# One row-tile block per chunk for all four strips, with the chunk's outputs in one run and PSUM banks chosen as the order is laid

## The chip, the cores and the metric

The kernel runs on one core of one Trainium2 chip. The metric is the device time of one execution in microseconds (us); lower is better. Work is spread over TensorE (PE, matmuls), VectorE (DVE), ScalarE (ACT), GpSimd (POOL) and the DMA queues, most of them issued by SyncE (SP). TensorE's products go to PSUM, which has eight banks of 512 float32 columns for 128 partitions.

## The reference

Four batches of 12800 rows with 128 channels pass an attention with 32 inducing points, twice (`mab`), and then a gated product with a causal depthwise convolution of five taps.

```python
def mab(q, kv):
    s = scale * (q @ kv.transpose(0, 2, 1))
    s = s - s.max(-1, keepdims=True)
    a = np.exp(s)
    a /= a.sum(-1, keepdims=True) + 1e-09
    return a @ kv
h = mab(I, x)          # I: the 32 inducing rows, softmax over the 12800 rows
x = mab(x, h)          # each row: softmax over 32 scores, then a @ h
...
for k in range(K):     # K = 5
    gate_pre += conv_w[k][None, None, :] * xp[:, k:k + S, :]
gate = 1.0 / (1.0 + np.exp(-gate_pre))
val = x @ w_val
return (gate * val @ w_out).astype(np.float32)
```

## The kernel before

**Tiling.** Each batch's 12800 rows are cut into four strips of 3200, and all strips are cut alike into chunks along the free dimension: eight chunks in batch 0 (128, 256, five of 512, 256 columns), seven in each other batch (448 and 480; batch 3 has 480, five of 512, 160). The 29 chunks are numbered 0 to 28 through the batches (`seqs`).

**Stages.** For each batch: first scores (`s1`, L422), maxima (`gm`), x transposed on TensorE where needed (`x`, L397), exponentials and sums of exp times x (`h`, L486), normalisation and folding of h into the weights (`u`, `t`, `w`, `W`, `po`; L528, L545, L565, L621, with cg, wf and w on GpSimd at L580 to L587). Then for each chunk: second scores (`s2`, L691) and their softmax over 32 (DVE, POOL and ACT), which ends in P1 and P2, the two float16 halves of the probabilities; GpSimd writes the second (L749, the P low half), with `sub` (L708) and `nm` (L731) before it. Since P has 32 values for a row, the gate and the value of a chunk are products of P with folded weights W of 32 x 128: for each strip fifteen gate matmuls (five taps, three products of halves each, L763) into a gate buffer in PSUM and three value matmuls (L772) into an 'a' bank. These are **row tiles**: the four strips lie on the four groups of 32 partitions and run beside each other. Scores and sums are **column tiles** (128 x 32), and outputs use the **full array**.

**After a block.** ScalarE takes the tanh of a pair of strips out of the gate buffer (tg, L833); VectorE multiplies it with the value in PSUM (gv, L843); ScalarE casts to a float16 half gh (L856), GpSimd takes the rest gl (L861); an output (`o`) is three full-array matmuls gh x wo, gh x wo, gl x wo (L884 to L886), for chunk 28 one in float32 (L877), then an eviction on VectorE (L899) or ScalarE (L901), by the list OUTV, and a store from SP (L920; L908 for chunk 28) or ACT (L914).

**Half blocks.** `rblock(k, half)` lays two half blocks for a chunk. In a half, one pair of strips (`ends`) finishes its gates while the other pair (`other`) does its three value units and begins its next gates; how many is chosen by a small dynamic programme (`begun`, with EVEN). A half that has values is written as two operations (`part(False)`, `part(True)`). There are 60 halves. The outputs of the pair that finished stand between halves.

**PSUM.** g0 and g1, the gate buffers of the two pairs, take two banks each with one buffer; the four 'a' banks hold scores, sums, values and outputs in turn: the k-th 'a' tile takes the bank of the (k-4)-th.

**The order.** Nothing is issued as it is written. Each step records an operation with its engine, an assumed duration, what it depends on and which tiles it makes and uses. ORDER, a list found by search, fixes TensorE's order. `lay` then lists the other engines' operations by assumed times, latest start first, shifted by a number for each function (URGE). `AHEAD` says how far loads run ahead, BUFS how many buffers each tile has. ("z", n, k) in ORDER stands for k matmuls of zeros into g1 (`idle`, L939), and eight more run at the start (L928, `warm_up`).

Of the kernel before, what the change touches and what calls it, by code (L numbers as in the profile page):

```python
# [20 lines left out]
P = 128  # L21
M = 32
R = 4
# [26 lines left out]
class Plan:  # L50
# [28 lines left out]
    def order(self, pe):  # L79
# [4 lines left out]
        for tag, made in self.tiles.items():  # L84
            bufs = BUFS[tag]
# [41 lines left out]
        for _ in range(PASSES):  # L127
            seq, at, end = self.lay(deps, succ, topo, nominal)
            if best is None or max(end) < best[0]:
                best = max(end), seq, at, end  # L130
            nominal = {b: end[a] for a, b in zip(pe, pe[1:])} | {pe[0]: 0.0}
        _, seq, self.at, self.end = best
# [3 lines left out]
    def lay(self, deps, succ, topo, nominal):  # L136
# [4 lines left out]
        for i in reversed(topo):  # L141
            late[i] = nominal.get(i, late[i])
            for s in succ[i]:
                late[i] = min(late[i], late[s] - ops[i]["dur"] - ops[i]["lag"])
        free, bus = {}, 1.45
# [9 lines left out]
        while len(seq) < n:  # L155
            best = None
            for e, lst in pools.items():
                if not lst:
                    continue
                start = max(free.get(e, 0.0), min(r for r, _ in lst))  # L160
                if best is None or start < best[0]:
                    best = (start, e)
# [6 lines left out]
            free[e] = end[i] - OVER.get(e, 0.0)  # L169
            if e == "SP":  # L170
                bus = max(bus, start) + ops[i]["dur"]
                end[i] = max(bus, start + 0.5) + (1.7 if start < 10.0 else 2.6)
                free[e] = start + 0.45
            seq.append(i)
# [9 lines left out]
        return seq, at, end  # L184


@functools.lru_cache(None)
def begun(n, units, even):


    last = len(n) - 1
    ways = {a: (a * n[0] + even * n[0] * (a - 6) ** 2, [a]) for a in range(units + 1)}
    for k in range(len(n)):
        more = {}
        for a, (c, way) in ways.items():
            for b in range(units + 1):
                first = max((units - a) * n[k], (3 * n[k - 1] if k else 0) + b * n[k]) + even * n[k] * (b - 6) ** 2
                for d in range(units + 1) if k < last else (0,):
                    second = max((units - b) * n[k], 3 * n[k] + (d * n[k + 1] if k < last else 0))
                    v = c + first + second + (even * n[k] * (d - 6) ** 2 if k < last else 0)  # L200
                    if d not in more or v < more[d][0]:
                        more[d] = v, way + [b, d]
        ways = more
    return min(ways.values())[1]
# [8 lines left out]
def tile_kernel(ctx: ExitStack, tc: tile.TileContext, xt, xk, indT_in, w64, out):  # L213
# [103 lines left out]
    def pt(key, shape=(P, 512), dt=F32):  # L317
        t = st[key] = psum.tile(list(shape), dt, name=key[0], tag=key[0], bufs=BUFS[key[0]])
# [457 lines left out]
    made = set()  # L776
# [330 lines left out]
```

## Time and profile before

| | us |
|---|---|
| three timed runs | 285.78, 286.11, 285.9 (median 285.9) |
| span of the profiled execution, first to last instruction | 284.3 |
| TensorE busy in it | 276.2 (97%) |
| VectorE, ScalarE, GpSimd busy | 232.2, 203.2, 214.0 |

The profiled execution has no timed duration of its own beside its span; the median of the timed runs is 1.6 us above it. Matmuls overlap, so a matmul's own duration is longer than the step from one to the next; the distance of two starts is what a matmul costs TensorE. The idle time in brackets is what an engine waited before a row, and the arrow names what ended it.

### The profile page before, as it was taken

To read this page: it belongs to the slowest core of one execution; us is meant where nothing else is said; L and a number is where in the kernel's file an instruction comes from. 1 tells how busy PE (TensorE), PEld (TensorE's weight loads), DVE (VectorE), ACT (ScalarE), POOL (GpSimd) and SP (SyncE) were. 2 spreads that over 40 slices of the span, in tenths; PEclk is the share of its full clock that TensorE was granted. 3 is DMA by queue.
4 is the path that set the end of the run, shared out by engine and by line. 5 is a ranking of instruction groups with operands and counts; after the bars stand their busy time and mean duration, and the time that the engine had idled before them with its cause. 6 is when DMAs were issued, how large, how long until landed. Compare 5 with 4: busy or idle time off the path is not lost.

```text
span 284.3 us, 9991 instructions
## 1 busy us (share of the span) xinstructions
PE 276.2 (97%) x4028; PEld 136.5 (48%) x4028; DVE 232.2 (82%) x577; ACT 203.2 (71%) x307; POOL 214.0 (75%) x256
## 2 busy tenths in 40 slices
PE   8899899999999999999999999999999999999992
PEld 3576547564343445555446445554444444333451
DVE  1694799999999989798898989877999977964571
ACT  2466162686884979787867599797778987888772
POOL 1122076998988789988798998989979979965680
PEclk9999999999999999999999999999999999999999
DMA  7999999979999879895999943144331343434445
GB/s 295 419 424 416 418 415 390 420 275 382 367 384 293 315 253 369 294 367 165 389 369 352 343 145 136 53 147 146 129 132 67 135 166 113 151 146 173 151 177 195
DMA packets 24351, 74.49 MB, mean 262 GB/s; under 512 B 2801, under 2 KB 12529, under 8 KB 22129
## 3 DMA queue, kind: packets, MB, share of 16 engines
q1 hardware_dynamic: 23872, 73.32, 68.2%
q8 instruction: 31, 0.51, 0.7%
q10 hardware_dynamic: 432, 0.54, 0.5%
q14 instruction: 16, 0.12, 0.1%
HBM read 47.63 MB, written 26.21 MB: 260 GB/s over the span
## 4 chain that ended last, share of the span: by engine, by line
PE 94%; DVE 2%; issue 1%; ACT 1%; POOL 0%; POOLq 0%
PE g L763 30%; PE a L884 9%; PE a L486 9%; PE a L691 8%; PE a L422 8%; PE a L772 8%; PE a L886 7%; PE a L885 7%; PE g L397 2%; PE g L939 2%; PE a L928 1%; PE a L621 1%; DVE ss L430 1%; PE a L528 1%; DVE os L899 0%
## 5 line engine op out<-in xcount | busy, mean ns | idle before, releaser
L861 POOL TENSOR_TENSOR gl<-tg,gh 128x1024 f16<-128x1024 f32 (+4 forms) x56 | 106.6, 1907 | 18.0 <-ACT gh L856 12.3
L763 PE MATMUL g<-P,W 32*128 32x448 f16 (+5 forms) x1740 | 109.7, 345 | 0.0
L833 ACT ACTIVATE tg<-g,gsc 128x1024 f32<-128x1024 f32 (+5 forms) x58 | 57.7, 995 | 32.3 <-PE g L763 29.0
L843 DVE SCALAR_TENSOR_TENSOR tg<-tg,a 128x512 f32<-128x512 f32 (+5 forms) x116 | 65.7, 603 | 10.2 <-PE a L772 8.7
L763 PEld LDWEIGHTS <-W 32*128 32x128 f16 x1740 | 51.0, 92 | 43.0 <-issue 13.2
L856 ACT CAST gh<-tg 128x1024 f16<-128x1024 f32 (+4 forms) x56 | 52.7, 942 | 0.8 <-PE a L885 0.8
L772 PE MATMUL a<-P,W 32*128 32x512 f16 (+5 forms) x348 | 43.1, 348 | 0.1
L901 ACT ACTIVATE os<-a,osc 128x448 f32<-128x448 f32 (+4 forms) x60 | 36.5, 632 | 6.2 <-PE a L886 5.7
L884 PE MATMUL a<-gh,wo 128*128 128x512 f16 (+4 forms) x112 | 40.1, 359 | 0.0
L885 PE MATMUL a<-gh,wo 128*128 128x512 f16 (+4 forms) x112 | 39.6, 354 | 0.0
L886 PE MATMUL a<-gl,wo 128*128 128x512 f16 (+4 forms) x112 | 39.6, 354 | 0.0
L899 DVE TENSOR_SCALAR os<-a,osc 128x448 f32<-128x448 f32 (+4 forms) x48 | 31.4, 670 | 9.6 <-PE a L886 9.4
L749 POOL TENSOR_TENSOR P<-pt,P 128x512 f16<-128x512 f32 (+4 forms) x29 | 29.9, 1037 | 1.8 <-ACT P L742 1.8
L731 POOL TENSOR_TENSOR e<-e,z 128x512 f32<-128x512 f32 (+4 forms) x29 | 27.1, 940 | 4.0 <-DVE z L723 2.8
L708 POOL TENSOR_TENSOR e<-e,m 128x512 f32<-128x512 f32 (+4 forms) x29 | 27.1, 939 | 3.9 <-DVE m L702 3.4
L486 PE MATMUL a<-xk,et 128*32 128x129 f32 x800 | 28.2, 275 | 0.7 <-DVE et L470 0.5
L422 PE MATMUL a<-xt,indT 128*32 128x512 f32 (+5 forms) x232 | 27.3, 538 | 0.0
L486 PEld LDWEIGHTS a<-xk,et 128*32 128x32 f32 x800 | 23.0, 109 | 8.6 <-issue 4.2
L691 PE MATMUL a<-xt,hT 128*32 128x512 f32 (+4 forms) x232 | 26.8, 544 | 0.0
L714 ACT ACTIVATE e<-e 128x512 f32<-128x512 f32 (+4 forms) x29 | 16.5, 572 | 10.6 <-POOL e L708 10.5
L430 DVE TENSOR_SCALAR_CACHE_REDUCE ss<-a 128x512 f32<-128x512 f32 (+5 forms) x29 | 17.1, 601 | 7.3 <-PE a L422 7.1
L884 PEld LDWEIGHTS <-wo 128*128 128x128 f16 x112 | 10.9, 97 | 25.0 <-issue 18.2
(108 smaller groups left out, 323.7 us busy)
## 6 DMA issues: line engine op xcount, KB each, us to landing
xt<-in_xt_dram SPq DMA_DIRECT2D x11, 1024.0 KB, 8.3
out_dram<-os SPq DMA_DIRECT2D x36, 256.0 KB, 3.6
xk<-in_xk_dram SPq DMA_DIRECT2D x10, 903.0 KB, 8.5
out_dram<-os SPq DMA_DIRECT2D x40, 224.0 KB, 2.6
xt<-in_xt_dram SPq DMA_DIRECT2D x8, 896.0 KB, 7.4
xk<-in_xk_dram SPq DMA_DIRECT2D x6, 1032.0 KB, 9.1
xt<-in_xt_dram SPq DMA_DIRECT2D x6, 960.0 KB, 7.8
xk<-in_xk_dram SPq DMA_DIRECT2D x5, 967.5 KB, 6.6
```

What stands on the lines that cost most here:

```text
L422: T.matmul(s[32 * r:32 * r + 32, :n], c_["indT"], x[:, o:o + n // 32, r, :], start=True, stop=True)
L486: T.matmul(t[32 * s:32 * s + 32, :P + 1], e[:, 32 * i:32 * i + 32], x[:, m + i, :], start=i < R, stop=i >= nb - R)
L691: T.matmul(s[32 * r:32 * r + 32, :n], st["hT", b], x[:, m:m + nb, r, :], start=True, stop=True)
L763: T.matmul(st[f"g{r // 2}", b, c][:, r % 2, :n], st["W", b][q, w, k, :], st[("P1", "P2")[e]][q, o:o + n], start=u == 0, stop=u == len(taps ...
L772: T.matmul(st["a", "v", b, c, r][:, :n], st["W", b][q, w, TAPS, :], st[("P1", "P2")[e]][q, o:o + n], start=u == 0, stop=u == 2)
L833: S.activation(t[:, :, :n], st[f"g{p}", b, c][:, :, :n], AF.Tanh, scale=st["gsc", b])
L843: V.scalar_tensor_tensor(t, t, 1.0, st["a", "v", b, c, r][:, :n], ALU.add, ALU.mult)
L856: S.copy(sb(pw, g1, [P, 2, 512], F16)[:, :, :n], st[tg][:, :, :n])
L861: G.tensor_tensor(sb(pw, g2, [P, 2, 512], F16)[:, :, :n], st[tg][:, :, :n], st[g1][:, :, :n], ALU.subtract)
L884: T.matmul(t, w[:, 0], st[g1][:, q, :n], start=True, stop=False)
L885: T.matmul(t, w[:, 1], st[g1][:, q, :n], start=False, stop=False)
L886: T.matmul(t, w[:, 0], st[g2][:, q, :n], start=False, stop=True)
```

## The change

- `rblock(k, *starts)` lays **one block for a chunk**, with the fifteen gate units of all four strips. The value units of the chunk before stand inside it: for the first pair of strips after `starts[0]` gate units, for the second after `starts[1]`. The block is cut at these places into operations of their own. Both tanh of the chunk come after the block's end. There are 30 blocks.
- An **'a' bank is chosen while the order is laid**: `lay` keeps a list of open banks with the time at which each comes free, gives a TensorE operation the earliest, and holds the operation back if there are too few.
- ORDER, URGE (now with a number for every function) and OUTV are new tables. The four outputs of a chunk stand mostly together. Twenty of the 21 matmuls of zeros stand in the middle of the order.
- AHEAD 25 to 12; buffers: xt 11 to 10, tg 3 to 4, gh 2 to 4, gl 2 to 3.
- The instructions are otherwise the same in kind and number, apart from two evictions that go from VectorE to ScalarE and one store that goes from SP to ACT.

```diff
+        wants = [[] for _ in range(n)]
+        held = {}
+        holds = [[] for _ in range(n)]
+        for i, key in self.tiles.get("a", []):
+            wants[i].append(key)
+            held[key] = 1 + len(self.users[key])
+            for u in [i] + self.users[key]:
+                holds[u].append(key)
+        open_ = [(0.0, b) for b in range(BUFS["a"])]
...
+                if e == "PE":
+                    w = len(wants[lst[0][1]])
+                    if w > len(open_):
+                        continue
+                    if w:
+                        start = max(start, open_[w - 1][0])
...
-        tag=key[0], bufs=BUFS[key[0]])
+        tag = f"a{plan.bank[key]}" if key[0] == "a" else key[0]
...
-    def rblock(k, half):
-        ends, other = ((0, 1), (2, 3)) if half == 0 else ((2, 3), (0, 1))
-        cur = seqs[k] if 0 <= k < len(seqs) else None
-        val = (seqs[k - 1] if k else None) if half == 0 else cur
-        nxt = cur if half == 0 else (seqs[k + 1] if k + 1 < len(seqs) else None)
...
+    def rblock(k, *starts):
+        cur = seqs[k] if k < len(seqs) else None
+        val = seqs[k - 1] if k else None
+        line = {r: [(gate_mm, *cur, r, u) for u in range(len(taps))] if cur else [] for r in range(R)}
+        cuts = [0, len(taps)]
+        if val:
+            for r in range(R):
+                at = starts[r // 2] if cur else 0
+                line[r][at:at] = [(val_mm, *val, r, u) for u in range(3)]
+            cuts = [0] + [at + d for at in sorted(starts) for d in (0, 3)] + [len(line[0])] if cur else [0, 3]
...
+        for lo, hi in zip(cuts, cuts[1:]):
+            todo = [line[r][s] for s in range(lo, hi) for r in range(R)]
...
+            i = PE(max(spent), f, list(dict.fromkeys(deps)), new, use, "rows", 0.34)
...
 ORDER = [
...
-    ("o", 26, 0), ("r", 28, 0), ("o", 26, 2), ("o", 26, 3), ("r", 28, 1), ("r", 29, 0), ("o", 28, 0), ("o", 27, 1),
...
+    ('o', 25, 0), ('o', 24, 1), ('o', 25, 2), ('r', 28, 6, 12), ('o', 25, 1), ('o', 26, 1), ('r', 29, 1, 12),
...
-AHEAD = 25
+AHEAD = 12
-BUFS = dict(xt=11, ..., tg=3, gh=2, gl=2, ...
+BUFS = dict(xt=10, ..., tg=4, gh=4, gl=3, ...
```

ScalarE near the end of the program, before (tanh L833 of one pair of a chunk of 512, cast to gh L856, output eviction L901; g_ and a number is one gate buffer):

```order
L856 CAST gh<-tg 128x1024
L833 ACTIVATE tg<-g_5290,gsc 128x1024
L901 ACTIVATE os<-a,osc 128x512 x2
L856 CAST gh<-tg 128x1024
L833 ACTIVATE tg<-g_5349,gsc 128x1024
```

And ScalarE there after (the same three operations are L827, L850 and L895):

```order
L827 ACTIVATE tg<-g_5337,gsc 128x1024
L827 ACTIVATE tg<-g_5340,gsc 128x1024
L850 CAST gh<-tg 128x1024
L895 ACTIVATE os<-a,osc 128x512 x2
L850 CAST gh<-tg 128x1024
L827 ACTIVATE tg<-g_5483,gsc 128x1024
L827 ACTIVATE tg<-g_5470,gsc 128x1024
```

The two tanh of a chunk now follow each other, and the casts and evictions stand between the chunks.

GpSimd around the first chunks of batch 0, before (cg, wf and w: the folding of weights; e: the scores in the softmax, sub at L708 and nm at L731; m and ng: maxima of batch 1; P: the low half):

```order
L580 TENSOR_SCALAR cg<-w,gs 128x5
L581 TENSOR_TENSOR wf<-hT,cg 128x160
L587 TENSOR_TENSOR w_592<-wf,w_592 128x160
L708 TENSOR_TENSOR e<-e,m_599 128x256
L708 TENSOR_TENSOR e<-e,m_642 128x160
L456 TENSOR_SCALAR m_644<-m_644 64x1
L457 TENSOR_SCALAR m_644<-m_644 32x1
L450 TENSOR_SCALAR ng<-m_644 32x1 x4
L731 TENSOR_TENSOR e<-e,z 128x256
L731 TENSOR_TENSOR e<-e,z 128x160
L708 TENSOR_TENSOR e<-e,m_712 128x512
L749 TENSOR_TENSOR P_95<-pt,P_94 128x256
```

And after (qm, u and osc: the scale of batch 0's outputs):

```order
L585 TENSOR_SCALAR cg<-w,gs 128x5
L586 TENSOR_TENSOR wf<-hT,cg 128x160
L713 TENSOR_TENSOR e<-e,m_566 128x160
L592 TENSOR_TENSOR w_570<-wf,w_570 128x160
L713 TENSOR_TENSOR e<-e,m_579 128x256
L736 TENSOR_TENSOR e<-e,z 128x160
L461 TENSOR_SCALAR qm<-qm 64x1
L462 TENSOR_SCALAR qm<-qm 32x1
L657 TENSOR_SCALAR u<-qm 32x1 x4
L658 TENSOR_SCALAR osc<-u 128x1
L713 TENSOR_TENSOR e<-e,m_671 128x512
L754 TENSOR_TENSOR P_117<-pt,P_116 128x160
```

The first chunk (128 columns and the strips' 32 leading ones, 160 together) now goes first, one nm stands behind the first low half instead of ahead of it, and the maxima of batch 1 have changed places with the output scale of batch 0.

TensorE at the end of the thirteen matmuls of zeros, before (in the start, between the transposes of batch 0's weights and its second scores):

```order
L939 LDWEIGHTS zero
L939 MATMUL g_688<-zero 128x512
L691 MATMUL a<-xt,hT 32x512 x8
L486 MATMUL a<-xk,et 32x129 x28
L763 LDWEIGHTS W
L763 MATMUL g_786<-P_94,W 128x128
```

And after (between two outputs of chunk 14, the first of batch 2):

```order
L933 LDWEIGHTS zero
L933 MATMUL g_3960<-zero 128x512
L878 LDWEIGHTS wo
L878 MATMUL a<-gh,wo 128x480
L879 LDWEIGHTS wo
L879 MATMUL a<-gh,wo 128x480
```

The run of thirteen has gone from the wait for batch 0's weights to the middle of the program.

## Rows read from the trace of the kernel before

**Rows 1.** The page's busy times (us, share of the span, instructions), and its chain that ended last by engine.

```profile
PE 276.2 (97%) x4028; PEld 136.5 (48%) x4028; DVE 232.2 (82%) x577; ACT 203.2 (71%) x307; POOL 214.0 (75%) x256
...
PE 94%; DVE 2%; issue 1%; ACT 1%; POOL 0%; POOLq 0%
```

**Rows 2.** Windows of the span: its length, then the busy us (and instructions) of PE, weight loads, DVE, ACT and POOL, the granted clock of TensorE, the DMA share and GB/s.

```profile
60.00:100.00 40.00, 40.00 (x592) 17.34 (x584) 38.50 (x99) 30.06 (x46) 34.67 (x36) 1.00 0.94 342
...
165.00:272.00 107.00, 107.00 (x1502) 46.98 (x1496) 85.55 (x174) 88.66 (x122) 91.63 (x77) 1.00 0.37 133
272.00:284.30 12.30, 7.21 (x80) 4.17 (x70) 5.47 (x11) 5.44 (x10) 4.23 (x3) 1.00 0.54 198
```

**Rows 3.** TensorE's timeline around a half block of 448 columns and the outputs on both sides: start, us, engine, line, what it does, count.

```profile
199.41 0.35 PE L885 MATMUL a<-gh,wo 128*128 128x448 f16 x1
199.60 0.35 PE L886 MATMUL a<-gl,wo 128*128 128x448 f16 x1
199.88 0.36 PE L763 MATMUL g<-P,W 32*128 32x448 f16 x2
...
201.70 0.36 PE L884 MATMUL a<-gh,wo 128*128 128x448 f16 x1
...
202.94 0.36 PE L772 MATMUL a<-P,W 32*128 32x448 f16 x2
```

**Rows 4.** TensorE's timeline where second scores (column tiles) end: sixteen of them, the output behind them, and eight before a block.

```profile
204.76 1.92 PE L691 MATMUL a<-xt,hT 128*32 128x512 f32 x16
206.62 0.36 PE L884 MATMUL a<-gh,wo 128*128 128x448 f16 x1
...
210.81 1.06 PE L691 MATMUL a<-xt,hT 128*32 128x512 f32 x8
211.80 0.36 PE L772 MATMUL a<-P,W 32*128 32x448 f16 x2
```

**Rows 5.** Groups of instructions of one shape over the whole span: count, busy us, mean ns of one, idle us of the engine just before them and what ended it.

```profile
L843 DVE SCALAR_TENSOR_TENSOR tg<-tg,a 128x512 f32<-128x512 f32 x40 | 25.7, 678 | 6.0 <-PE a L772 5.7
...
L833 ACT ACTIVATE tg<-g,gsc 128x1024 f32<-128x1024 f32 x20 | 22.3, 1113 | 12.5 <-PE g L763 12.4
L856 ACT CAST gh<-tg 128x1024 f16<-128x1024 f32 x20 | 20.8, 1042 | 0.4 <-PE a L885 0.4
...
L901 ACT ACTIVATE os<-a,osc 128x512 f32<-128x512 f32 x20 | 13.2, 684 | 2.9 <-PE a L886 2.9
...
L899 DVE TENSOR_SCALAR os<-a,osc 128x512 f32<-128x512 f32 x16 | 11.7, 744 | 6.7 <-PE a L886 6.7
```

**Rows 6.** TensorE's timeline in the start: two s1 chunks, the normalisation of batch 0 (L528), the folding (L545, L565), the zeros, and the first row tiles.

```profile
27.09 1.88 PE L422 MATMUL a<-xt,indT 128*32 128x448 f32 x16
...
32.06 0.82 PE L528 MATMUL a<-H,D 128*32 128x129 f32 x6
32.81 0.60 PE L939 MATMUL g<-zero 128*128 128x512 f16 x2
33.77 0.21 PE L545 MATMUL a<-identf,hn 32*128 32x32 f32 x1 [0.35 <-DVE hn L536]
34.27 0.41 PE L565 MATMUL a<-hT,w 128*128 128x32 f32 x2 [0.28 <-DVE hT L548]
...
38.08 2.98 PE L939 MATMUL g<-zero 128*128 128x512 f16 x13
...
44.59 0.51 PE L763 MATMUL g<-P,W 32*128 32x128 f16 x12
```

**Rows 7.** GpSimd's timeline in the start: cg, the two nm, the sub of a 512-column chunk, the first two low halves of P, and osc.

```profile
35.05 0.27 POOL L580 TENSOR_SCALAR cg<-w,gs 128x5 f32<-128x5 f32 x1 [7.82 <-DVE vmx L592]
...
40.16 1.03 POOL L731 TENSOR_TENSOR e<-e,z 128x256 f32<-128x256 f32 x2
41.15 1.05 POOL L708 TENSOR_TENSOR e<-e,m 128x512 f32<-128x512 f32 x1
43.42 1.12 POOL L749 TENSOR_TENSOR P<-pt,P 128x256 f16<-128x256 f32 x2 [1.22 <-ACT P L742]
...
50.00 0.22 POOL L653 TENSOR_SCALAR osc<-u 128x1 f32<-128x1 f32 x1
```

**Rows 8.** The matmuls of zeros by their line (ns least, median and most, first and last start), and the eight of the warm-up in TensorE's timeline.

```profile
L939 PE MATMUL g<-zero x21: 377/379/534, 4.6 to 40.7; 128*128 128x512 f16 x21
...
1.17 3.59 PE L928 MATMUL a<-zero 128*128 128x512 f16 x8 [1.17 <-DVE warm L240]
```

**Rows 9.** The timeline of all engines at the end: tanh, the block behind it, GpSimd's last two low halves, the last outputs, the last eviction of 512 columns and the last store.

```profile
270.24 1.11 ACT L833 ACTIVATE tg<-g,gsc 128x1024 f32<-128x1024 f32 x1 [0.50 <-PE g L763]
...
271.47 0.24 PE L763 MATMUL g<-P,W 32*128 32x160 f16 x2
...
273.33 4.22 POOL L861 TENSOR_TENSOR gl<-tg,gh 128x1024 f16<-128x1024 f32 x2 [1.33 <-PE a L885]
...
278.92 0.44 PE L877 MATMUL a<-tg,wof 128*128 128x160 f32 x2
...
280.12 0.38 SPq L908 DMA_DIRECT2D out_dram<-ss  x1
```

More of the change, by code (lines that the diff above doesn't have):

```diff
@@ L127, in order @@
         for _ in range(PASSES):
[L128 removed]
+            seq, at, end, bank = self.lay(deps, succ, topo, nominal)
             if best is None or max(end) < best[0]:
[L130 removed]
+                best = max(end), seq, at, end, bank
             nominal = {b: end[a] for a, b in zip(pe, pe[1:])} | {pe[0]: 0.0}
[L132 removed]
+        _, seq, self.at, self.end, self.bank = best
         self.alldeps = deps
@@ L169, in lay @@
             free[e] = end[i] - OVER.get(e, 0.0)
+            for key in wants[i]:
+                bank[key] = open_.pop(0)[1]
             if e == "SP":
@@ L173, in lay @@
                 free[e] = start + 0.45
+            for key in holds[i]:
+                held[key] -= 1
+                gone[key] = max(gone.get(key, 0.0), end[i] + (ops[i]["lag"] if e != "PE" else 0.0))
+                if not held[key]:
+                    open_.append((gone[key], bank[key]))
+                    open_.sort()
             seq.append(i)
@@ L183, in lay @@
                     pools.setdefault(ops[s]["eng"], []).append((avail[s], s))
[L184 to L204, printed above, removed]
+        return seq, at, end, bank
 def cost(kind, n):
@@ new lines, in rblock @@
+    def rblock(k, *starts):
[8 more added lines that the diff above has]
+            cuts = [0] + [at + d for at in sorted(starts) for d in (0, 3)] + [len(line[0])] if cur else [0, 3]
+        seen, done, i = set(), {}, None
+        for lo, hi in zip(cuts, cuts[1:]):
+            todo = [line[r][s] for s in range(lo, hi) for r in range(R)]
+            deps, new, use, spent = [], [], [], [0.0] * R
+            for fn, b, c, r, u in todo:
@@ L816, in f @@
+                if (b, c) == cur:
+                    deps.append(ix["P", b, c])
+            def f(todo=todo):
                 for fn, *a in todo:
                     fn(*a)
-            return PE(max(spent.values()) - before + 0.02, f, deps, new, use, "rows", 0.34)
-        i0 = part(False) if val else None
-        i = part(True)
+            i = PE(max(spent), f, list(dict.fromkeys(deps)), new, use, "rows", 0.34)
+            for fn, b, c, r, u in todo:
+                if u == 2 and fn is val_mm:
+                    done[r] = i
@@ L847, in rblock, with gv @@
-            if (b, c) != seqs[-1]:
-                halves(b, c, p)
+            for p in sorted(range(2), key=lambda p: starts[p]):
+                for r in (2 * p, 2 * p + 1):
+                    def gv(b=b, c=c, p=p, r=r, n=SIZES[b][c]):
+                        t = st["tg", b, c, p][:, r % 2, :n]
+                        V.scalar_tensor_tensor(t, t, 1.0, st["a", "v", b, c, r][:, :n], ALU.add, ALU.mult)
+                    ix["gv", b, c, r] = op("DVE", cost("psum", SIZES[b][c]), gv, [done[r], ix["tg", b, c, p]], 0.0, [],
+                                           [("tg", b, c, p), ("a", "v", b, c, r)])
+                if (b, c) != seqs[-1]:
+                    halves(b, c, p)
```

153 lines of the change are left out of this document (84 added, 69 removed), and 81 rows, old and new, of tables (ORDER, OUTV).

## The prediction

> **What bounds the kernel now.** I read the page's busy times and its chain of waits first [rows 1]: TensorE (PE) is busy for 276.2 of 284.3 us and 94% of the chain that ended last lies on it, so the time is what TensorE executes plus what it waits. Then the table of windows [rows 2]: from 60 to 272 us TensorE is busy for every microsecond of each stretch, so there a microsecond of its work taken out is one gained, as long as nothing else is late. What could be late differs by stretch: VectorE (DVE) has 38.5 of the 40 us up to 100, so a block that asks more of it there will wait; after 165 ScalarE, VectorE and GpSimd (POOL) stand at 80 to 86%, and it is single waits, not an engine's sum, that could hold TensorE. Two stretches are not bounded by TensorE's work: the wait for batch 0's weights (38 to 41, filled by thirteen matmuls on zeros [rows 6]) and the end after 279 us, which is eviction and store [rows 9].
>
> The sum is made against the profiled span, 284.3; the three timed runs have the median 285.9, 1.6 more, and I carry this 1.6 over unchanged.
>
> **Term 1, fewer changes of tiling.** TensorE runs in three ways here: full array (outputs), row tiles (blocks) and column tiles (scores, sums). Each change costs a little, and the timeline shows it [rows 3]: one 448-column step follows another after .19 us (199.41 to 199.60), but from the last output matmul to the first row tile it is .28, so .09 is the change; nine steps of row tiles at .19 are 1.71, and the block takes 1.82 (199.88 to 201.70), so the way back costs .11; six output steps 1.14 against 1.24, .10. For column tiles [rows 4]: sixteen score matmuls take 1.86 until the next kind starts, eight take .99, so eight take .87 and the change .12. Going through the order, I count 165 changes before and 118 after. By kind: rows to full 28 fewer (x .11), full to rows 11 fewer (x .09), column tiles to rows 18 fewer (x .12), full to column tiles 3 fewer (x .10), one less from rows to column tiles, and column tiles to full 14 more (x .12): 3.1 + 1.0 + 2.2 + .3 + .1 - 1.7 = **-5.0**.
>
> **Term 2, the blocks themselves.** A block lasts as long as its slowest strip. At .19 per 448 columns the units of the slowest strips sum to 99.6 us before and 98.5 after: the half blocks lost where two chunk sizes met, the whole ones lose less. **-1.1**. The instructions are the same, and where an instruction stands in a longer run costs nothing that [rows 3] show.
>
> **Term 3, the matmuls on zeros.** There are 21 in both. Before, all start by 40.7 us [rows 8], thirteen of them in the wait for weights, 2.98 [rows 6]. After, one stands early and twenty in the dense part: two behind batch 1's folded weights, thirteen between the outputs of chunk 14, one and four in batch 3. At 2.98 / 13 = .23 and, by the steady step at 512 columns, .217 each, this is 20 x .217 = **+4.3**. If TensorE would wait at these places anyway, they cost nothing: 0 to +4.3. I take the whole, because [rows 2] show no wait there now and the neighbouring outputs need chunk halves that the order leaves time for.
>
> **Term 4, the start.** Two s1 chunks of 448 fewer stand ahead of batch 0's normalisation (1.88 [rows 6]), so its last matmul ends near 30.9 instead of 32.8. GpSimd begins cg 2.3 us after it (35.05 [rows 7]), so at 33.2. Ahead of the first P low half the GpSimd queue holds nearly the same work as before, which took 7.15 (35.05 to 42.20): one nm of 256 columns fewer (some .55 of the 1.03 for two), osc (.22) more, and .4 less waiting: 6.4 to 6.8. The low half itself takes .56 (1.12 for two). So block 0 can start at 40.1 to 40.7, where before it was 44.59. But TensorE has little until then. From 34.27 to 38.08 it did 3.8 of work; one s1 chunk less (.94) and one score chunk more (about .9) leave 3.8, and with the small transposes and their waits it is done at 35.5: idle for 4.6 to 5.2, and some .6 again before block 1, which needs the tanh of block 0 and the second chunk's P. Before, the zeros lay in such waits: .60 + 2.98 = 3.6. Against 5.0 this is **+1.4**, with -.5 and +2.5 as ends: the lower if the GpSimd queue waits as little as its neighbours, the upper if VectorE's reductions come as late as in 60 to 100.
>
> **Term 5, new waits in the middle.** A whole block writes both gate buffers, so both tanh must end before the next block begins its gates, and val needs all four 'a' banks. Between blocks TensorE has other work, so this costs only where that work is shorter than the end of a matmul (.36 - .19 = .17) and two tanh (2 x 1.11 [rows 5]) = 2.4. With four outputs of .65 (three steps of .19 x 512 / 448 = .217) and two changes between blocks it is 2.8: .4 to spare. By my count seven places have .2 to .4 (before blocks 11, 12, 23, 26, 27, 28 and 29), all others over .6. The nearest row is in the drain of before: a tanh ends at 271.35 (270.24 + 1.11) and the block that needs its buffer begins at 271.47 without a wait [rows 9], with .12 to spare. So the value is near nothing: **+.3**, ends 0 and +2.5. Queued behind a late tanh on ScalarE are casts to gh, behind these GpSimd's low halves and the next outputs; one more tg and two more gh buffers let them run ahead. Two evictions move from VectorE (.744) to ScalarE (.684): nothing, with 20% of either free after 165.
> The Trainium skill ("TensorEngine Tiling (Array Packing)", PSUM Bottleneck) says that tiling speeds up TensorE but not the emptying of PSUM; that speaks against a longer row block with all four banks, and is rival 1. [Rows 2] bear it out only up to 100 us, where VectorE is full.
>
> **Term 6, the end.** In the last block the vals of both pairs of chunk 27 now come together, so GpSimd's two low halves (4.22 [rows 9]) stand behind one block: from its start 1.2 to the first val's end, gv 1.3 (2 x .678), cast 1.04 [rows 5], then 4.3, some 8 us, against 7 us of TensorE work: about 1 waited. In return 512-column stores go last, straight behind their eviction; before it was a 160-column one, issued 1.0 after TensorE's end (278.92 + .24 to 280.12). **-.3**, ends -.8 and +1.
>
> **Sum.** -5.0 - 1.1 + 4.3 + 1.4 + .3 - .3 = -.4: a span of 283.9, a median of **285.5**. Its own range, by terms 4 and 6 and half of term 3's doubt: 284.3 to 286.7.
>
> **Rivals.**
> **1, two tanh and PSUM set the pace (slower).** Place: the seven thin places, above all blocks 23 to 28, where only outputs stand between blocks. If ScalarE starts a cast (1.04 [rows 5]) just before a block ends, the second tanh is that much later, and 1.04 less .3 to spare is .7 of TensorE idle. It decides as soon as a cast is taken ahead of the tanh at more than one of them: three places give 2.1, 287.6; all seven 4.9. For it: ScalarE's queue has a cast or an eviction beside each tanh. Against it: tanh before waited for TensorE, not for ScalarE (12.4 of 12.5 idle [rows 5]).
> **2, the zeros and the start cost nothing (faster).** If TensorE waits at the zeros' places anyway, or half of them, and the start is like before, 4.3 goes to about 2.2 and 1.4 to 0: 285.5 - 3.5 = 282.0 at best, about 282.9 in the middle. For it: thirteen zeros stand where batch 3's start would make TensorE wait for hn. Against it: outputs lie beside them that need nothing of it.
> **3, the clock (slower).** The start leaves TensorE idle for up to 5 us in pieces without the zeros. The clock row shows the full level, 2.4 GHz, in every slice of before, but the first eight matmuls of the program, after 1.17 idle, took .42 each against .22 later [rows 8]. If the first 4 to 8 us after the gap go at half speed, that is +1.8 to +3.6, some 288.
> The Trainium skill ("TensorE: Matmul & The Clock Gate", Part 1: The HAM clock gate) has it that throttled is the default, activity releases it and idleness brings it back; no row of before shows a fall.
> **4, the change doesn't do what it says.** If the cost of a change of tiling is hidden where blocks are cut into several operations, or the bank choice forces waits that equal it, term 1 is lost: 290.5.
>
> **How the numbers follow.** The forecast has .41 (by its range and the bound of .2%, about what a measurement of this kernel can tell from no change, 285.3 to 286.5: .18 faster, .17 same, .06 slower), rival 1 .25 (.02 same, .23 slower), rival 2 .24 (faster), rival 3 .06 and rival 4 .04 (slower). Faster .42, same .19, slower .39. The range takes in most of rivals 1 and 2 and half of rival 3: 282.7 to 288.4; outside are the lower end of rival 2 (.08), all seven places of rival 1 (.05), and rivals 3 and 4 (.07).
>
> **What would show it.** Term 1: row-tile groups half as many, steps still .19, and the .09 to .12 at each change. Term 3: twenty matmuls on zeros after 90 us, each a step of .22 with no wait ended behind them; a wait at their side makes it rival 2. Term 4: the first row tile at 40 to 41 with some 5 us idle ahead. Term 5 and rival 1: TensorE idle with a gate matmul released by ScalarE's tanh, at blocks 11, 12 and 23 to 29. Term 6: two low halves back to back behind the last val. Rival 3: a clock below 1.00 between 36 and 50. It would be wrong if VectorE cannot follow up to 100 us, where the blocks come four microseconds earlier than before and its row is already full.

## The result

The changed kernel takes 289.2 us (four runs, 288.4 to 290.08) against 286.0 for the kernel before in the same measurement: 1.0104 of it, 95% interval 1.0074 to 1.0133. It is slower, by 3.0 us, where 285.5 had been forecast with a range of 282.7 to 288.4. The later runs shared other measurements, in which the kernel before took 286.6 to 286.9, so they are given as ratios to it; .0035 is 1 us.

The page of the changed kernel, busy times and the chain that ended last (compare [rows 1]):

```profile
PE 272.6 (95%) x4028; PEld 139.9 (49%) x4028; DVE 232.0 (80%) x575; ACT 204.7 (71%) x309; POOL 213.9 (74%) x256
...
PE 77%; DMA 13%; DVE 5%; POOL 1%; ACT 1%; issue 1%; ACTq 0%; DVEq 0%
```

TensorE has 3.6 us less of busy time, yet the span is 288.3 and not 284.3; 13% of the chain now lies on DMA. Where the time went, by windows (columns as in [rows 2]):

```profile
34.00:60.00 26.00, 21.80 (x448) 12.28 (x452) 22.90 (x71) 15.12 (x30) 19.84 (x35) 0.93 0.71 262
60.00:100.00 40.00, 39.78 (x552) 19.09 (x545) 36.09 (x96) 32.54 (x51) 34.45 (x45) 1.00 0.81 308
100.00:165.00 65.00, 63.68 (x1055) 34.16 (x1052) 55.45 (x137) 46.98 (x72) 50.49 (x52) 1.00 0.91 338
...
200.00:272.00 72.00, 72.00 (x954) 31.72 (x954) 59.46 (x118) 58.01 (x78) 61.87 (x51) 1.00 0.37 132
272.00:288.30 16.30, 10.58 (x122) 5.89 (x120) 8.21 (x16) 8.13 (x14) 8.49 (x4) 0.94 0.63 230
```

The kernel before in two of these stretches:

```profile
34.00:60.00 26.00, 25.73 (x476) 14.39 (x476) 25.15 (x81) 14.19 (x30) 19.66 (x40) 1.00 0.96 386
...
100.00:165.00 65.00, 65.00 (x1011) 33.98 (x1014) 58.41 (x152) 48.93 (x79) 57.53 (x71) 1.00 0.87 318
```

Three things are to be seen. From 34 to 60 TensorE is idle for 4.2 us, against .3 before, and its granted clock is .93. From 100 to 165 it waits for 1.3 us, with the DMA share up from .87 to .91. From 200 to 272, where rival 1 had put most of its thin places, it is busy for all 72 us: no tanh holds it. (The .94 of the last stretch comes from behind TensorE's last matmul.) The start in TensorE's timeline (compare [rows 6]):

```profile
32.18 0.21 PE L550 MATMUL a<-identf,hn 32*128 32x32 f32 x1 [0.98 <-DVE hn L541]
...
34.61 0.57 PE L626 MATMUL a<-ident,w 128*32 128x128 f16 x24 [0.69 <-ACT w L590]
...
38.34 0.24 PE L768 MATMUL g<-P,W 32*128 32x128 f16 x4 [1.11 <-ACT P L747]
40.53 1.68 PE L768 MATMUL g<-P,W 32*128 32x128 f16 x56 [1.95 <-POOL P L754]
42.14 1.72 PE L427 MATMUL a<-xt,indT 128*32 128x448 f32 x8
...
47.37 1.69 PE L427 MATMUL a<-xt,indT 128*32 128x448 f32 x16
```

Block 0 issues its first four matmuls at 38.34 and the others at 40.53, when the P low half has come. Then eight first-score matmuls take as long (1.72 at 42.14) as sixteen do five microseconds later (1.69 at 47.37): half speed. Windows of one microsecond show it, in the column ahead of the DMA share:

```profile
40.00:41.00 1.00, 0.47 (x20) 0.47 (x23) 0.71 (x3) 0.85 (x2) 1.00 (x3) 0.77 1.03 432
41.00:42.00 1.00, 1.00 (x48) 0.95 (x36) 0.91 (x2) 0.59 (x2) 1.00 (x2) 0.50 0.97 396
42.00:43.00 1.00, 1.00 (x16) 0.20 (x8) 0.56 (x3) 0.76 (x2) 1.00 (x3) 0.50 1.03 432
43.00:44.00 1.00, 1.00 (x18) 0.21 (x14) 0.07 (x1) 0.79 (x3) 0.89 (x2) 0.52 1.00 417
```

The clock stands at its lower level, 1.2 GHz, from 40.5 to 44, and about 1.75 us are lost. TensorE had been idle for 3.1 us of the 3.3 from 37.2 to 40.5, in the two waits of 1.11 and 1.95.

The zeros by their line (compare [rows 8]), then three of the sums in TensorE's list of waits (us in total, times, longest), then the row of ScalarE's timeline that stands behind the third:

```profile
L933 PE MATMUL g<-zero x21: 376/379/608, 5.3 to 224.5; 128*128 128x512 f16 x21
```

```profile
PE a L491 <- DMA xk<-in_xk_dram: 1.3, 1, 1.3
...
PE a L427 <- DMA xt<-in_xt_dram: 0.9, 1, 0.9
...
PE a L626 <- ACT os L895: 0.6, 1, 0.6
```

```profile
170.91 0.63 ACT L895 ACTIVATE os<-a,osc 128x448 f32<-128x448 f32 x1 [1.10 <-DMA out_dram<-os]
```

The first two are loads that come late, at 123.7 and at 18.5. (The one at 18.5 costs nothing against the kernel before: ahead of 30 us TensorE's idle time sums to 2.4 us in both.) Behind the third is an eviction, at 170.9, that waits until an older store has landed and its buffer is free. The end (compare [rows 9]):

```profile
276.36 0.22 PE L777 MATMUL a<-P,W 32*128 32x160 f16 x1 [0.17 <-DVE tg L837]
...
277.02 0.38 PE L777 MATMUL a<-P,W 32*128 32x160 f16 x10 [0.44 <-DVE os L893]
...
277.83 0.38 PE L878 MATMUL a<-gh,wo 128*128 128x512 f16 x1 [0.42 <-DVE tg L837]
```

TensorE waits here for a bank (.44) and for gv, 1.0 us in the brackets and 1.2 by the distances of starts, not for GpSimd's low halves.

### The profile page after: what moved, and what is told of

It reads as the page before. It is cut to its first block, busy times and chain, and to the rows that moved or that the text cites. A ratio compares the mean times of both kernels' runs of the same rounds, so it can differ in the third digit from the quotient of the medians.

```text
span 288.3 us, 9918 instructions
## 1 busy us (share of the span) xinstructions
PE 272.6 (95%) x4028; PEld 139.9 (49%) x4028; DVE 232.0 (80%) x575; ACT 204.7 (71%) x309; POOL 213.9 (74%) x256
## 4 chain that ended last, share of the span: by engine, by line
PE 77%; DMA 13%; DVE 5%; POOL 1%; ACT 1%; issue 1%; ACTq 0%; DVEq 0%
PE g L768 27%; PE a L878 8%; PE a L491 7%; PE a L696 7%; PE a L879 7%; PE a L880 7%; PE a L427 5%; PE a L777 5%; DMA xt<-in_xt_dram 5%; DMA out_dram<-os 4%; DMA xk<-in_xk_dram 3%; PE g L402 2%; PE g L933 2%; DMA indT<-in_indT_dram 1%; DVE tg L837 1%
## 5 line engine op out<-in xcount | busy, mean ns | idle before, releaser
L768 PE MATMUL g<-P,W 32*128 32x512 f16 (+5 forms) x1740 | 104.2, 348 | 3.1 <-POOL P L754 2.0
L837 DVE SCALAR_TENSOR_TENSOR tg<-tg,a 128x512 f32<-128x512 f32 (+5 forms) x116 | 64.3, 601 | 13.6 <-PE a L777 13.4
L768 PEld LDWEIGHTS <-W 32*128 32x128 f16 x1740 | 51.9, 94 | 45.9 <-issue 14.0
L850 ACT CAST gh<-tg 128x1024 f16<-128x1024 f32 (+4 forms) x56 | 52.3, 940 | 16.3 <-DVE tg L837 15.2
L827 ACT ACTIVATE tg<-g,gsc 128x1024 f32<-128x1024 f32 (+5 forms) x58 | 55.5, 991 | 8.7 <-PE g L768 7.0
L895 ACT ACTIVATE os<-a,osc 128x448 f32<-128x448 f32 (+4 forms) x61 | 38.0, 640 | 7.6 <-PE a L880 3.7
L777 PE MATMUL a<-P,W 32*128 32x512 f16 (+5 forms) x348 | 42.0, 345 | 0.6 <-DVE os L893 0.4
L878 PE MATMUL a<-gh,wo 128*128 128x448 f16 (+4 forms) x112 | 39.9, 357 | 0.6 <-DVE tg L837 0.4
L879 PE MATMUL a<-gh,wo 128*128 128x448 f16 (+4 forms) x112 | 39.5, 354 | 0.0
L880 PE MATMUL a<-gl,wo 128*128 128x448 f16 (+4 forms) x112 | 39.5, 354 | 0.0
L893 DVE TENSOR_SCALAR os<-a,osc 128x448 f32<-128x448 f32 (+4 forms) x47 | 30.7, 672 | 3.8 <-PE a L880 3.1
L491 PEld LDWEIGHTS a<-xk,et 128*32 128x32 f32 x800 | 23.8, 109 | 8.7 <-DVE tg L837 3.3
```

The source lines that it names most:

```text
L491: T.matmul(t[32 * s:32 * s + 32, :P + 1], e[:, 32 * i:32 * i + 32], x[:, m + i, :], start=i < R, stop=i >= nb - R)
L768: T.matmul(st[f"g{r // 2}", b, c][:, r % 2, :n], st["W", b][q, w, k, :], st[("P1", "P2")[e]][q, o:o + n], start=u == 0, stop=u == len(taps ...
L777: T.matmul(st["a", "v", b, c, r][:, :n], st["W", b][q, w, TAPS, :], st[("P1", "P2")[e]][q, o:o + n], start=u == 0, stop=u == 2)
L827: S.activation(t[:, :, :n], st[f"g{p}", b, c][:, :, :n], AF.Tanh, scale=st["gsc", b])
L837: V.scalar_tensor_tensor(t, t, 1.0, st["a", "v", b, c, r][:, :n], ALU.add, ALU.mult)
L850: S.copy(sb(pw, g1, [P, 2, 512], F16)[:, :, :n], st[tg][:, :, :n])
```

## The experiments

All times are ratios to the kernel before, with their 95% intervals. The changed kernel is 1.0104.

### The zeros, planned anew

```diff
 zeros_front, zeros_out:
-    ('z', 5, 2) ... ('z', 2, 13) ... ('z', 0, 1) ... ('z', 1, 4)
 zeros_front, zeros_both:
+    ('u', 0), ('z', ., 4), ('t', 0), ('w', 0), ('z', ., 1), ... ('z', ., 2), ('W', 0, 0), ... ('z', ., 13), ('r', 0),
 touch (nine of these between outputs):
+            T.matmul(pt(("a", "y", k))[:, :2], c_["zero"][:32, :P], c_["zero"][:32, :2], start=True, stop=True)
```

> The changed kernel with its twenty matmuls on zeros taken out of the middle and put into the start: four behind batch 0's normalisation, one and two around its folded weights, thirteen ahead of block 0. My theory: in the middle they cost their full step, 20 x .217 = 4.3 us, and in the start they hold TensorE's clock at full level, where the changed kernel showed .50 from 41 to 44 us, some 1.75 lost. So 289.2 - 4.3 - 1.75, about 283 us, faster than before by 1%, and a granted clock of 1.00 in every stretch. Rival (the zeros in the middle stand where TensorE would wait anyway): only the clock comes back, 287.5, and the waits of TensorE behind chunk 14 grow by 2.8.

> The changed kernel without these twenty matmuls on zeros, put nowhere else. My theory: 4.3 us less, about 284.9, and the clock still falls to .50 for some 3.5 us behind the wait for block 0. Rival (they fill waits): 289.2, no change, with new idle of TensorE where they stood.

> The changed kernel with twenty more matmuls on zeros in the start, and those in the middle kept. This is the clock alone. My theory: the clock stays at 1.00 between 36 and 46 us and 1.75 come back: 287.4. Rival (the clock's fall hides behind waits for VectorE and GpSimd, which have the same work at any clock): 289.2, the same.

> The changed kernel with nine row-tile matmuls of two columns, on zeros into an 'a' bank of their own, each in the middle of a run of outputs between blocks 18 and 28; each adds two changes of tiling and next to no work. My theory (a change costs .09 to .11): 9 x .20 = 1.8 us more, 291.0, and in the timeline two steps of about .28 where they stand. Rival (term 1 was wrong and a change is hidden where the engine has loads ahead): no more than .2, 289.4.

Measured: zeros_front 1.0218 (1.0194 to 1.0241), zeros_out 1.0104 (1.0076 to 1.0131), zeros_both 1.0186 (1.0155 to 1.0216), touch 1.0388 (1.0364 to 1.0412). All four miss what the first theory gave. The rival gives the number of zeros_out (no change), but not those of the others: by it none was to be slower than the changed kernel by more than .2 us. An edit of ORDER has the program laid anew, and 196, 113, 155 and 75 of the 337 'a' tiles got another bank, the other engines another order. In zeros_front and touch that brought, among others, these waits of TensorE:

```profile
PE a L777 <- DVE tg L837: 2.3, 3, 1.7
...
PE a L626 <- ACT os L895: 1.3, 1, 1.3
```

```profile
250.07 0.61 PE L768 MATMUL g<-P,W 32*128 32x512 f16 x4 [3.76 <-POOL P L754]
```

Behind the long wait of touch the clock falls as well, to .92 on average from 250 to 270. So these runs show what a new layout is worth, not what a zero or a change of tiling costs. The following keep the layout.

### The same edits in the changed kernel's own layout

```diff
-    def idle(k, n):
+    def idle(k, n, real=None):        # planned as n, issued as real
 mute, moved:
-    ('z', 2, 13)                      # and the other three alike
+    ('z', 2, 13, 0)
 moved, warm:
+    ('z', 6, 0, 4), ... ('z', 7, 0, 1), ... ('z', 8, 0, 2), ... ('z', 9, 0, 13), ('r', 0),
 touch2, ahead of an output's matmuls:
+                if 4 * k + r in TOUCH:
+                    T.matmul(t[:, :2], c_["zero"][:32, :P], c_["zero"][:32, :2], start=True, stop=True)
```

> The changed kernel with exactly its own order on every engine and its own 337 bank choices; only the twenty matmuls on zeros in the middle are not issued (the planner still reckons with their time). In the runs before, taking them out let the planner lay the program anew: 113 to 196 of 337 'a' banks were others, and the new layouts waited elsewhere. Theory A (the zeros cost their step, new layouts have new bank waits): 4.3 us less than the changed kernel, 1.0104 - .015, about .995 of the kernel before. Theory B (TensorE has to wait there for the other engines): no more than 1 us less, 1.007, with new idle of TensorE behind the places.

> As the run with the zeros not issued, and twenty zeros issued in the start, with no time reckoned for them, so that order and banks stay those of the changed kernel. Theory A: another 1.75 us less, since the clock does not fall behind the wait for block 0: .989 of the kernel before, and a granted clock of 1.00 from 36 to 46. Theory B: the clock's 1.75 alone, 1.004.

> Order and banks of the changed kernel, its zeros in the middle kept and twenty more issued in the start: the clock alone. Theory A: 1.75 us less than the changed kernel, 1.004 of the kernel before. Theory B (what runs at half clock there is hidden by waits for VectorE): 1.010, no change.

> Order and banks of the changed kernel, with a row-tile matmul of two columns on zeros ahead of 27 outputs between blocks 18 and 28, into the output's own bank, which the output then overwrites; each adds two changes of tiling. In the run with nine of them in banks of their own the layout was another and one block waited 3.8 us for a bank, so its +8 us say little of a change's price. Theory A (a change costs .09 to .11): 27 x .20 = 5.4 us more than the changed kernel, 1.029 of the kernel before, steps of about .28 around each. Theory B (hidden by loads ahead): under 1 us, 1.013.

Every engine's order and all 337 banks are those of the changed kernel. (The long wait of the run touch was for a P low half, as its row shows, and not for a bank, as the last expectation says.)

**warm**: 1.0016 (.9996 to 1.0037), 2.5 us less with the same work and twenty matmuls more. The clock column from 40 to 42 reads 1.00:

```profile
40.00:42.00 2.00, 1.99 (x68) 1.06 (x68) 1.59 (x6) 1.53 (x5) 2.00 (x3) 1.00 1.05 422
```

Theory A holds: with the gaps filled the clock stays up and time comes back. The 2.5, which the two intervals leave open by about 1.0, are .7 more than the half clock's 1.75, and they need not all be the clock's: from 50 to 270 TensorE is idle for .8 us in warm's profile against 2.1 in the changed kernel's, since it waits less for loads and not at 171.

**mute**: 1.0051 (1.0025 to 1.0077), 1.5 us less. **moved**: .9973 (.9954 to .9993), 1.2 less than warm; it is faster than the kernel before. Twenty steps are 4.3 us, so about a third of it arrives: between the two theories. About half of what is missing shows in moved at block 17, behind the place of the thirteen zeros, in TensorE's and ScalarE's timelines:

```profile
190.60 0.66 ACT L895 ACTIVATE os<-a,osc 128x480 f32<-128x480 f32 x1
...
191.31 0.34 PE L777 MATMUL a<-P,W 32*128 32x448 f16 x1 [0.99 <-ACT os L895]
...
192.29 0.34 PE L777 MATMUL a<-P,W 32*128 32x448 f16 x1 [0.64 <-DVE os L893]
```

The values wait for two banks of chunk 14's outputs, whose evictions stand behind softmax work. (Chunk 14 is the last chunk of batch 1; that it is the first of batch 2, as the section on the change has it, is a slip, and so is the block 18 of a later expectation. The expectations' 1.06 and .70 are these two waits by the distances of starts.) Where the other half went isn't traced.

**touch2**: 1.0265 (1.024 to 1.0291), 4.6 us for 27 places. Its timeline:

```profile
242.81 0.37 PE L882 MATMUL a<-gl,wo 128*128 128x480 f16 x1
243.11 0.17 PE L879 MATMUL a<-zero 32*128 32x2 f16 x1
243.21 0.38 PE L880 MATMUL a<-gh,wo 128*128 128x480 f16 x1
243.43 0.37 PE L881 MATMUL a<-gh,wo 128*128 128x480 f16 x1
```

From 242.81 to 243.21 it is .40 where a step of 480 columns is .20: .20 for the two changes, with whatever the small matmul itself needs. So a change costs at most .10, in line with term 1 (.09 and .11). In the profile TensorE loses 5.7 us on the changed kernel between 206 and 276, where the 27 places stand, .21 for each; the timed 4.6 agree with that within what the intervals leave open, about 1.1.

### The banks, and the zeros of the kernel before

```diff
 rotemit, rotemit_moved (tiles as issued; every order kept), rot_moved (planned so too):
-        tag = f"a{plan.bank[key]}" if key[0] == "a" else key[0]
-        t = st[key] = psum.tile(list(shape), dt, name=key[0], tag=tag, bufs=1)
+        t = st[key] = psum.tile(list(shape), dt, name=key[0], tag=key[0], bufs=BUFS[key[0]])
 before_mute (the kernel before, with the same idle(k, n, real)):
-    ("z", 5, 2) ... ("z", 2, 13)
+    ("z", 5, 2, 0) ... ("z", 2, 13, 0)
```

> The changed kernel with every engine's order as it is, but the 'a' tiles take their banks in turn, as before, and not as chosen while the order was laid. It undoes the choice of banks alone. Theory A (the choice keeps TensorE from waiting for an eviction that is laid late): slower than the changed kernel by 1 to 4 us, 1.014 to 1.024 of the kernel before, with new waits of value and output matmuls for DVE or ACT evictions. Theory B (the choice does nothing, four banks come free in turn anyway): 1.010, the same. Theory C (the choice is what costs, since it fixes banks by reckoned times that the chip does not keep): faster, 1.003.

> The same edit on the kernel with the zeros moved into the start (.9973 of the kernel before). There block 18 waited 1.06 and .70 us for banks whose evictions stood behind softmax work in ACT's and DVE's queues. Theory A: 1.002 to 1.012, with more such waits. Theory B: .997. Theory C: .993, without the waits at block 18.

> The kernel with the zeros moved into the start, planned anew with banks in turn, so that the other engines' orders are laid for them. If a layout that reckons with turns is as good as one with chosen banks, .997; if one block for four strips needs the choice, 1.005 or more, by waits of values for banks.

> The kernel before in its own order, with fifteen of its zeros in the start (two behind batch 0's normalisation, thirteen in the wait for its weights) not issued. They fill waits, so leaving them out can only cost by the clock. Theory A: the granted clock falls to .50 somewhere between 36 and 48 us, and the time grows by 1.5 to 2.5 us, 1.005 to 1.009. Theory B (the fall in the changed kernel came from something else than the idle time): the same, 1.000.

rotemit 1.0093 (1.0065 to 1.0121), rotemit_moved .9994 (.9971 to 1.0018): with all orders kept, these runs tell no difference between banks in turn and chosen ones, theory B. The choice matters while the order is laid: rot_moved, laid for turns, is 1.0512 (1.0487 to 1.0537), with 3.3 us of waits of values for ScalarE's evictions alone. This ORDER was searched with the choice, so it doesn't tell what turns could reach.

before_mute 1.0000 (.9985 to 1.0015), a miss for theory A. Without these fifteen zeros the kernel before is idle for 1.69 of the 2 us from 40 to 42, and keeps its clock:

```profile
38.00:40.00 2.00, 2.00 (x44) 0.58 (x32) 1.93 (x6) 1.05 (x3) 1.58 (x6) 1.00 1.00 414
40.00:42.00 2.00, 0.31 (x12) 0.23 (x12) 1.89 (x7) 1.66 (x3) 1.85 (x5) 1.00 1.04 408
42.00:44.00 2.00, 1.88 (x58) 1.64 (x51) 2.00 (x6) 1.80 (x5) 0.78 (x2) 1.00 1.00 410
```

So this gap did not lower the clock; the changed kernel's long gap has 3.1 us of idle time. It has short ones too, between 30 and 36. The next runs take the short and the long apart.

### Which gap, which wait, and the end

```diff
 moved13 / moved7: of moved's zeros only the thirteen ahead of block 0 / only the seven ahead of them
 late17, in rblock, the first pair of block 17:
+        for r in LATE.get(k, ()):
+            real[r].sort(key=lambda w: w[0] is val_mm)      # values behind all gates
 tail1:
-    ('r', 29, 1, 12), ('o', 26, 0), ('o', 28, 0),
+    ('o', 26, 0), ('r', 29, 1, 12), ('o', 28, 0),
```

> As the kernel with the zeros moved into the start, but only the thirteen ahead of block 0 are issued, not the seven between 31 and 35 us. Theory A (any idle of 3 us and more in a short stretch lets the clock fall): it falls to .50 near 36 to 38, as in the run with no zeros in the start, and 1 to 2 us are lost: 1.001 to 1.004. Theory B (only the long gap ahead of block 0 does it): clock 1.00, .997.

> The counterpart: only the seven zeros between 31 and 35 us are issued, not the thirteen ahead of block 0. Theory A: the clock falls to .50 at 40 to 44, 1.5 to 2 us lost, 1.002 to 1.004. Theory B, the long gap ahead of block 0 alone does it: the same here. If the clock stays at 1.00, the two gaps together make it fall: .997.

> The kernel with the zeros moved into the start (.9973 of the kernel before), with one edit: in block 17 the first pair's twelve value matmuls are issued behind all its gates and not behind six of fifteen units. In the middle of that block TensorE waited 1.06 and .70 us for two banks whose evictions stand behind softmax work in ACT's and DVE's queues; before the change of the zeros, thirteen of them ran there. Theory A (the zeros filled a wait for banks, so taking them out could not give their 4.3 us): the wait shrinks or goes, and 1.0 to 1.7 us come back, .992 to .994. Theory B (the time is set by the softmax and eviction queues, and the wait only moves to the next block): .997.

> The kernel with the zeros moved into the start, with the last values (block 29) one output later in the order. In the end TensorE waited .24, .50 and .49 us there, for banks held by outputs. If this is what the end lost, .5 to 1.0 us less: .994 to .996. If the end hangs on GpSimd's two last low halves, nothing: .997.

moved7, with the long gap open, 1.0065 (1.0041 to 1.009); moved13, with the short ones open, 1.0003 (.9982 to 1.0023). In moved7 the clock falls behind the long gap:

```profile
38.00:40.00 2.00, 0.24 (x4) 0.10 (x4) 1.93 (x6) 0.32 (x1) 1.73 (x6) 1.00 1.04 435
40.00:42.00 2.00, 1.19 (x60) 0.99 (x63) 1.60 (x6) 1.19 (x3) 2.00 (x4) 0.85 1.01 419
42.00:44.00 2.00, 2.00 (x23) 0.55 (x24) 1.10 (x4) 1.69 (x5) 2.00 (x4) 0.50 0.98 407
```

In moved13's profile it stays at 1.00 from 30 to 46, though TensorE is idle for 2.0 us between 30 and 36. So the long gap, ahead of block 0 and in it, is enough. But the short ones can be enough too. mute has the start of the changed kernel, and in its profile the clock falls behind the short gaps and is back ahead of the long one:

```profile
33.00:34.00 1.00, 0.32 (x18) 0.32 (x20) 0.96 (x7) 0.33 (x1) 0.73 (x3) 0.91 1.02 413
34.00:35.00 1.00, 1.00 (x21) 0.41 (x16) 0.96 (x4) 0.34 (x1) 0.80 (x3) 0.50 1.04 428
...
37.00:38.00 1.00, 1.00 (x12) 0.14 (x5) 0.72 (x2) 0.84 (x2) 0.74 (x4) 0.88 1.02 425
38.00:39.00 1.00, 0.13 (x4) 0.00 (x0) 0.99 (x2) 0.00 (x0) 1.00 (x2) 1.00 1.00 416
```

TensorE had been idle there for 1.9 us between 30.4 and 33.7, in three waits of .9, .3 and .7. The profiles of zeros_out and touch2, with the same start, show the fall at the same place; that of touch shows none in the start. And the eleven runs behind moved13's ratio fall into two groups by their mean granted clock: five at .998 to 1.000 take 286.1 us on average, six at .990 to .992 take 287.4. The profile is one of the five; of the six there is no trace, so where their clock fell is not shown. Its .0030 above moved, which lies at the edge of the intervals, comes from these six. So which gap lets the clock fall differs from run to run, and no profile with both filled shows a fall in the start. (moved13 left 2.0 us of idle time, less than its first theory had named, so it doesn't test that figure.)

late17 .9985 (.9962 to 1.0008), no gain: theory B. In its profile, of the slowest of its twelve runs (288.3, median 286.1), a wait of .16 is left in block 17 of 1.06 and .70, but others of the same kind stand elsewhere, one of them ahead of the edit:

```profile
179.53 0.34 PE L777 MATMUL a<-P,W 32*128 32x448 f16 x1 [0.56 <-DVE os L897]
...
200.85 0.34 PE L777 MATMUL a<-P,W 32*128 32x448 f16 x1 [0.29 <-ACT os L899]
207.48 0.35 PE L882 MATMUL a<-gh,wo 128*128 128x448 f16 x1 [0.76 <-DVE os L897]
```

So the wait in block 17 was one for banks, and could be moved; but taking it away did not shorten the program, and why is not settled beyond these rows.

tail1 1.0006 (.9987 to 1.0026), no gain: its values still wait .2 and .4, now at 273.75 and 274.41, and the first output of chunk 28 waits for gv. What the end lost doesn't hang on that one place; it is not settled further.

### The loads

```diff
 both: os 4 to 2, gh 4 to 3, H 4 to 3, D 6 to 4; xt11 also:
-BUFS = dict(xt=10,
+BUFS = dict(xt=11,
```

> The kernel with the zeros moved into the start, with eleven buffers for xt, as the kernel before had, and room made for it (os 4 to 2, gh 4 to 3, H 4 to 3, D 6 to 4), which lays the other engines anew. It is to be read against the next run, which has the same orders on TensorE, ACT, DVE and POOL. Theory A (the loads stop at 44 to 50 us for want of an xt buffer, and the DMA engines are full between 100 and 125, where TensorE waits up to 1.4 us for an xk load): the DMA share from 34 to 60 rises, the wait near 121 goes, and the run is .5 to 1.5 us faster than its pair. Theory B (loads come late by the order of the program, not by buffers): the same as its pair.

> The pair of the run with eleven xt buffers: the same smaller buffers os, gh, H and D, and ten xt buffers. Theory A: .5 to 1.5 us slower than its pair, with the wait for xk near 121 us. Theory B: the same as its pair. Against the kernel with the zeros moved (.9973) both may be slower by some us, since the new layout was not chosen.

xt11 1.1682 (1.1632 to 1.1731), xt10 1.1783 (1.1741 to 1.1825). The pair differs by 1%, in theory A's direction, but the medians of all six runs of each are 338.0 and 338.6, and on a program that has become 50 us longer this says nothing of the 1 us in question: inconclusive. Part of what made it longer shows in ScalarE's and VectorE's waits of xt10: with two os buffers, evictions wait for stores that have not landed.

```profile
ACT os L895 <- DMA out_dram<-os: 10.5, 9, 3.1
...
DVE os L893 <- DMA out_dram<-os: 7.5, 8, 2.1
```

The layout is another as well: 225 of the 337 'a' tiles got another bank.

The trace of the changed kernel tells more of the loads: the queue of SyncE, and the longest of its waits between 30 and 62.

```profile
33.98 3.65 SPq L364 DMA_DIRECT2D xt<-in_xt_dram  x3
49.76 1.97 SPq L914 DMA_DIRECT2D out_dram<-os  x4
51.82 3.80 SPq L364 DMA_DIRECT2D xt<-in_xt_dram  x2
```

```profile
SPq L914 <- ACT os L895: 12.1, 1, 12.1
```

From 37.7 to 49.76 the queue issues nothing. Next in it is a store, which waits 12.1 us for its eviction, and the loads stand behind the store. In the kernel before four xk loads go out between 43.82 and 48.51, ahead of the first store. With eleven xt buffers the queue stands in the same way: in xt11 nothing goes out from 38.0 to 48.59, and then a store does. So this pause comes from the order on SyncE, as theory B has it, and not from the buffers. AHEAD (25 to 12), which says how far loads run ahead, was not tried alone, and whether the pause is what makes the load at 123.7 late is not shown.

## Why the prediction was wrong, step by step

- **Terms 1 and 2 (changes of tiling and blocks, -6.1): right.** TensorE's steps, all distances of starts less the idle time and the zeros, sum to 270.1 us before and 266.2 after; the latter contain the 1.75 at half clock, so the work is 5.7 less (5.1 if the idle time is taken from the brackets). touch2 bears out the price of a change, at most .10.
- **Term 3 (the zeros, +4.3): half wrong.** They take 4.4 us of TensorE's steps, as reckoned, but out of the program they give back 1.5 (mute) or 1.2 (moved against warm). The step that failed is "I take the whole, because [rows 2] show no wait there now": rows of before can't show the waits of an order that is not theirs. Rival 2 was right in its mechanism; its place, as far as it is traced, was not hn but banks behind evictions: 1.6 us of waits in block 17.
- **Term 4 (the start, +1.4): its idle time was right, its price was not.** The changed kernel is idle for 5.8 us between 30.9 and 46.3 against .8 of idle and 3.6 of zeros before, +1.4, by the distances of starts (by the busy times of these windows 5.2 against .6 and 3.6, +1.0). But the start, unfilled, lets the clock fall. That is **the step that failed**: the clock stood beside the sum as rival 3 with a chance of .06, with 1.8 to 3.6 us and some 288, and it happened: 1.75 us by its length in the profile, and filling the gaps gave 2.5 back (warm). The argument for the small chance, that no row of before shows a fall, could not hold, since before has no such gap. Taking warm's 2.5 into the sum gives 288.0, still 1.2 short.
- **Term 5 (new waits, +.3): 2.3 us between 50 and 272,** inside its ends (0 to 2.5), but none is of the kind that was named: loads at 122 (1.4), the eviction behind a store at 171 (.6) and a wait of .3 at 76. Rival 1, the tanh, did not occur: TensorE is busy for 72.00 of 72.00 us from 200 to 272, and no row of its waits names a tanh. For the loads the sum had no term. The DMA share is .71 from 34 to 60 where it was .96, since SyncE's queue stands behind a store, and the bytes come later, when the share is .91; that this makes the later loads late is argued, not shown.
- **Term 6 (the end, -.3): +.7.** The wait came out as large as reckoned, 1.2 us against .2 before, but for gv and a bank; the low halves on GpSimd, which had been named, held nothing. What failed is the return: from TensorE's last matmul to the span's end it is .3 shorter, and -.3 in all, with 1 waited, would have needed about 1.3.

Summed over the profiled execution, by the distances of starts: -5.7 of work, +1.75 of half clock, +8.4 of idle time (11.0 against 2.6), -.3 at the end, -.3 for the zeros' own steps: +3.9, where the spans differ by 4.0.

With the clock kept and the middle zeros not issued (moved) the change is faster than the kernel before by .27%, interval .07 to .46%. That is the lowest ratio found here; three near relatives of it (late17, rotemit_moved, tail1) came out at .9985 to 1.0006, so the gain is small if it is one.

## What to carry to other kernels

When a change empties a stretch of TensorE, price the clock behind it as part of the sum, and fill all its gaps, the short ones too, with matmuls on zeros: here that gave back 2.5 us, of which the half clock explains 1.75. One profile does not tell which gap matters; look at the mean clock of every run too. When a schedule is computed, test an edit in the layout that stands, planned as before and issued otherwise: the same edit, planned anew, came out .5 to 2.5% slower, and told of the planner. Filler in the middle of a full engine is not all loss: see first what its neighbours wait for without it.

## What the runs showed of the hardware

- TensorE's granted clock fell from 2.4 to 1.2 GHz after 3.1 us of idle time within 3.3 (the changed kernel) and stayed at the lower level for 3.5 us. With the same start it fell in mute after 1.9 us within 3.3, in waits of which none was longer than .9, and stayed low from 33.8 to 37.2. It did not fall after 1.69 within 2.0 (before_mute), nor, in the profiled run, after 2.0 spread over 6 (moved13), where six other runs show a lower mean clock. The Trainium skill ("TensorE: Matmul & The Clock Gate", Part 1: The HAM clock gate) says that idleness brings the throttled state back; the trace agrees, .50 from 41 to 44.
- A row-tile matmul of two columns between two full-array matmuls costs .20 us, though it has next to no work.
- A store under load lands late: between 108 and 124 us, at a DMA share of 1.0, stores of 256 KB took 8.1 us (median) from issue to landing, where the last ones of before took 2.1 to 3.1. With two buffers for them, and fewer of three other kinds, the program is 17 to 18% longer, in another layout.
